# Final units of 256 successive tokens of one batch, stored in 4 KB rows, in an attention and spectral-mixing kernel

## Chip, cores, metric

One core of a Trainium2 chip. The metric is the device time of one execution in microseconds. The kernel before takes 451.3 us (median of 6 runs, 448.56 to 452.69).

## The reference, cut to what matters

```python
# attention: 8 batches, 8 heads, 576 tokens, window 128, ALiBi bias  ->  x [8, 576, 512]
X = rfft(x, axis=1)                      # 64 modes are kept
Y = X[:, :64] mixed per mode with w_r, w_i   # 64 x 2 matrices of 512 x 512 fp32: 134 MB
u = x + irfft(Y)
out = u + relu(u @ w_ch)                 # fp32, 9.44 MB
```

The engines are named as in the profile: PE multiplies matrices, ACT, DVE and GpSimd (POOL in the profile) work on elements, SP issues transfers (DMA). PSUM is the memory that PE writes its results to. The kernel has three stretches. Attention runs to about 130 us. Then the weights stream in and PE multiplies them with the spectra as they land; beside this, x is already projected with w_ch and kept as XW. After the last weight come 18 "final units" of 256 token rows each: `mm` gathers u @ w_ch, ACT takes the relu into `r`, `yy` gathers u, DVE adds the two into `o`, and SP stores `o`. In a "pooled" unit GpSimd adds x to `r`, so PE need not add it into `yy`.

## The kernel before

```python
units = []                                    # before: a unit is one tile of 128 tokens
for bp in range(B // 2):                      # of two batches, b and b + 1
    units += [(2 * bp, st) for st in range(FULL)]
    if bp % 2:
        units.append((2 * bp - 2, FULL))      # the 64 last tokens of four batches
...
def begin(j):                                 # brings XW into PSUM
    ...
        for row in range(2):
            nc.tensor.matmul(
                mm[ROWS[row], n], lhsT=ident[ROWS[n], ROWS[n]],
                rhs=XW[ROWS[n], j, row], start=True, stop=False, skip_group_check=True,
            )

def channels(j):                              # adds the high modes' channel rows
    ...
        for row in range(2):
            spread(mm[:, n], row, b + n, 1, st, row)

def spread(dst, half, b, hf, st, tok):
    row = ROWS[(b % 2) ^ (1 - hf)]            # the batch's parity picks the row half of PE
    nc.tensor.matmul(
        dst[ROWS[half]], lhsT=FT[row, b % 2, tokens(st, tok)], rhs=ZW[row, b // 2, hf],
        start=False, stop=True, skip_group_check=True,
    )
...
def activate(j):                              # begin, channels, relu; for pooled units
    ...                                       # GpSimd adds x to r
def finish(j):
    ...  # add_tokens(j) unless pooled (x through PE), finish_tokens(j), DVE add, store
        nc.sync.dma_start(
            out=out[b + c.start : b + c.stop, st * P : (st + 1) * P].rearrange(
                "b p e -> p b e"), in_=o[:, c])       # 2 KB rows
...
for step in ("a0 f0 a1 f1 a2 a3 f2 a7 f7 a9 a5 f3 f5 a4 f9 a6 a11 f6 f4 a10 a14 f10 "
             "a15 f11 a8 f14 f8 a13 f15 a16 f16 f13 a17 f17 a12 f12").split():
    {"a": activate, "f": finish}[step[0]](int(step[1:]))
```

In `begin` and `channels`, n picks the row half of the PE array and `row` the column half. The four 64x64 matmuls of each step thus lie in four different quadrants.

The softmax here doesn't subtract the row's maximum and nothing guards it: scores larger than these inputs give would overflow.

Of the kernel before, what the change touches and what calls it, by code (L numbers as in the profile page):

```python
# [10 lines left out]
FP32 = mybir.dt.float32  # L11
# [3 lines left out]
ALU = mybir.AluOpType  # L15
# [91 lines left out]
class _Attention:  # L107
# [71 lines left out]
    def inverse_table(self):  # L179

        nc = self.nc
        NM = self.F.shape[2] // 2
        for sts in (range(FULL), (FULL,)):
            ps = self.ps.tile([P, 2, 512], FP32, tag="sc", bufs=2)
            for par in range(2):
                for k in range(4):
                    c0 = NM // 2 * (k % 2) + NM * (1 - (k // 2 + par) % 2)
                    for st in sts:
                        n = P if st < FULL else TAIL
                        nc.tensor.matmul(  # L190
                            ps[32 * k : 32 * k + 32, par, st % FULL * P : st % FULL * P + n],
                            lhsT=self.F[:n, st, c0 : c0 + 32], rhs=self.ident[:n, :n],
                            start=True, stop=True, tile_position=(0, 32 * k),
                        )
            w = P * FULL if len(sts) > 1 else TAIL
            nc.scalar.copy(self.FT[:, :, sts[0] * P : sts[0] * P + w], ps[:, :, :w])
# [203 lines left out]
def kernel(  # L400
# [128 lines left out]
    with ExitStack() as mctx:  # L529
# [14 lines left out]
        def late_end(acc, g, n):  # L544
# [4 lines left out]
            patch([(nc.gpsimd, b) for b in range(2 if g == LAST else 0, B)],  # L549
# [70 lines left out]
        def tokens(st, half):  # L620
            o = st * P + (64 * half if st < FULL else 0)
            return slice(o, o + 64)

        def spread(dst, half, b, hf, st, tok):

            row = ROWS[(b % 2) ^ (1 - hf)]
            nc.tensor.matmul(  # L627
                dst[ROWS[half]], lhsT=FT[row, b % 2, tokens(st, tok)], rhs=ZW[row, b // 2, hf],
                start=False, stop=True, skip_group_check=True,
            )  # L630

        units = []
        for bp in range(B // 2):
            units += [(2 * bp, st) for st in range(FULL)]
            if bp % 2:
                units.append((2 * bp - 2, FULL))

        def token_tiles(j):
            b, st = units[j]
            return x[:, b : b + 2, st] if st < FULL else x[:, b + 1 : b + 4 : 2, FULL]  # L640
# [3 lines left out]
        def transposed(j):  # L644
            src = token_tiles(j)
            tr = lps.tile([P, 2, 4, P], BF16, tag="tr", name="tr")
            for n in range(2):
                for dt in range(4):
                    nc.tensor.transpose(tr[:, n, dt], src[:, n, dt * P : (dt + 1) * P], ident)  # L649
            xTs[j] = pool.tile([P, 2, 4, P], BF16, tag="xT", name="xT")  # L650
            nc.vector.tensor_copy(xTs[j], tr)  # L651
# [6 lines left out]
        def project(j):  # L658

            b, st = units[j]  # L660
# [4 lines left out]
            for n in range(2):  # L665
                mm = ps.tile([P, DM], FP32, tag="my", bufs=2, name="my")
                for dt in range(4):
                    for half in range(2):
                        lhsT = xT[:, half, dt, ROWS[n]] if st < FULL else xT[:, n, dt, ROWS[half]]
                        nc.tensor.matmul(  # L670
                            mm[ROWS[half]], lhsT=lhsT, rhs=wch[:, dt],
                            start=(dt == 0), stop=False, skip_group_check=True,
                        )
                mms.append(mm)
            for n in range(2):
                for half in range(2):
                    spread(mms[n], half, b + half + (2 * n if st == FULL else 0), 0, st, n)
            for n in range(2):
                nc.scalar.copy(XW[:, j, n], mms[n])  # L679
            if j + 1 < len(units):  # L680
                transposed(j + 1)

        POOLED, HALVES, FIRST = (3, 4, 9, 11, 13, 14, 15), (0, 1, 2, 3, 7, 12), (0, 1)
# [10 lines left out]
        def begin(j):  # L694
# [4 lines left out]
            for n in range(2):  # L699
                if units[j][1] == FULL:  # L700
                    nc.tensor.matmul(mm[:, n], lhsT=pairs, rhs=XW[:, j, n],
                                     start=True, stop=False, skip_group_check=True)
                    continue
                for row in range(2):
                    nc.tensor.matmul(  # L705
                        mm[ROWS[row], n], lhsT=ident[ROWS[n], ROWS[n]],
                        rhs=XW[ROWS[n], j, row], start=True, stop=False, skip_group_check=True,
                    )

        def channels(j):  # L710

            mm, b, st = mms[j][0], *units[j]
            for n in range(2):
                if st == FULL:
# [3 lines left out]
                for row in range(2):  # L718
                    spread(mm[:, n], row, b + n, 1, st, row)

        def last_rows(ps, j, rows):

            st = units[j][1]
            for n in range(2):
                nc.tensor.matmul(ps[:, n], lhsT=FM[:, n, st * P : (st + 1) * P], rhs=rows,  # L725
# [20 lines left out]
        def add_tokens(j):  # L746

            yy = yys[j][0]
            for n in range(2):
                nc.tensor.matmul(yy[:, n], lhsT=ident if units[j][1] < FULL else pairs,  # L750
                                 rhs=token_tiles(j)[:, n],
                                 start=True, stop=False, skip_group_check=True)

        def finish_tokens(j):

            yy, b, st = yys[j][0], *units[j]
            for n in range(2):
                if st < FULL:
                    nc.tensor.matmul(  # L759
                        yy[:, n], lhsT=FT[:, n, st * P : (st + 1) * P], rhs=Z[:, b + n],  # L760
# [9 lines left out]
        def finish(j):  # L770

            b, st = units[j]
            if j == 0:
                last_rows(yys[0][0], 0, heads["yq"])
# [6 lines left out]
            (yy, slot), r = yys.pop(j), rs.pop(j)  # L781
            o = heads["out"].tile([P, 2, DM], FP32, tag="o", bufs=5, name="o")
            for c in parts(j):
                nc.vector.tensor_tensor(out=o[:, c], in0=yy[:, c], in1=r[:, c], op=ALU.add)  # L784
                if st < FULL:
                    nc.sync.dma_start(
                        out=out[b + c.start : b + c.stop, st * P : (st + 1) * P].rearrange(
                            "b p e -> p b e"),
# [14 lines left out]
        for g in range(NM // 4):  # L803
# [5 lines left out]
            for i in range(8):  # L809
# [34 lines left out]
                if k == K1 - 1:  # L844
# [13 lines left out]
                    FM = right.tile([P, 2, 2 * P], BF16, name="FM")  # L858
                    nc.gpsimd.memset(FM, 0.0)
                    for b in range(2):  # L860
                        nc.gpsimd.dma_start(
                            out=FM.rearrange("(k v) b s -> k v b s", v=16)[:, b, b],
                            in_=FT[64 * b + 56 : 64 * b + 64, b, : 2 * P],
                        )
# [46 lines left out]
        patch([(nc.sync, 0), (nc.sync, 1)], yq, LAST, lambda b: Z[:, b])  # L911
        patch([(nc.sync, 2)] + [(nc.gpsimd, b) for b in (3, 4, 5, 6)], yq, LAST, lambda b: Z[:, b], 6)
# [17 lines left out]
        channel_rows([(nc.sync, 0), (nc.sync, 1)] + [(nc.gpsimd, b) for b in range(2, B)])  # L930
        patch([(nc.gpsimd, 7)], yq, LAST, lambda b: Z[:, b], 6)

        for step in ("a0 f0 a1 f1 a2 a3 f2 a7 f7 a9 a5 f3 f5 a4 f9 a6 a11 f6 f4 a10 a14 f10 "
                     "a15 f11 a8 f14 f8 a13 f15 a16 f16 f13 a17 f17 a12 f12").split():
# [31 lines left out]
```

## Time and profile before

| mark in the profiled run of the kernel before | us |
|---|---|
| start of the last tile's normalisation in x (taken as the end of attention) | 131.0 |
| first matmul of the last channel product, `zl` | 416.85 |
| first store issued | 420.48 |
| end of the last matmul | 443.75 |
| end of the span | 450.4 |

`zl` follows directly on the last weight, so "`zl` to the end" is the final stage: 33.55 us. Its marks, first from the chain that ended last (start, us, what), then from the order of time (start, us, engine, line, what):

```profile
416.85 1.15 PE zl L569 x8
...
420.48 16.80 SPq L786 DMA_DIRECT2D out_dram<-o  x17
...
445.02 1.27 SPq L786 DMA_DIRECT2D out_dram<-o  x2
```

The last row is the last pair of stores. The page, the windows and the chain of this kernel are shown in the prediction.

### The profile page before, as it was taken

How to read it: one execution, taken by the hardware profiler on the slowest of the kernel's cores; microseconds unless marked ns; L12 is line 12 of the kernel's file. 1: busy time of each engine (PE TensorE's matmuls, PEld its weight loads, DVE VectorE, ACT ScalarE, POOL GpSimd, SP SyncE). 2: the span in 40 equal slices, each digit the busy share in tenths (PEclk: the TensorE clock that was granted, in tenths of full speed). 3: DMA queues.
4: the chain of work that ended last, by engine and by line, in shares of the span. 5: the costliest groups of instructions: out<-in, count | busy, mean ns of one | idle time of the engine just before them, and what ended most of it. 6: DMA issues, size and time to landing. Idle time of an engine off the chain costs nothing. (4 is left out here: it accounts for less than half of the span.)

```text
span 450.4 us, 8021 instructions
## 1 busy us (share of the span) xinstructions
PE 362.3 (80%) x3314; PEld 193.1 (43%) x3314; DVE 177.0 (39%) x323; ACT 152.7 (34%) x196; POOL 73.9 (16%) x130
## 2 busy tenths in 40 slices
PE   4789899999968275776674766999999998877994
PEld 3457676777755032221222233544444443332331
DVE  7878699999752011010100132121212212220684
ACT  6859799999820000000000010211122110110772
POOL 8600000011512010200000000000000000054881
PEclk9989899999999659565659799999999999999998
DMA  8999999999999999999999999999999999995597
GB/s 282 310 310 319 302 232 303 321 311 263 212 266 319 316 260 314 326 372 427 418 421 421 423 422 419 420 421 420 421 418 421 421 420 421 420 399 206 197 358 295
DMA packets 53768, 157.03 MB, mean 349 GB/s; under 512 B 5205, under 2 KB 24421, under 8 KB 41317
## 3 DMA queue, kind: packets, MB, share of 16 engines
q1 hardware_dynamic: 47908, 140.56, 81.2%
q0 software_dynamic: 5824, 15.97, 18.1%
q8 instruction: 26, 0.43, 0.4%
q14 instruction: 10, 0.07, 0.0%
HBM read 162.53 MB, written 9.44 MB: 382 GB/s over the span
## 5 line engine op out<-in xcount | busy, mean ns | idle before, releaser
L832 PE MATMUL acc<-w,XC 128*32 128x512 bf16 x456 | 130.3, 451 | 42.5 <-DMA w<-in_moe_w_i_dram 22.1
L832 PEld LDWEIGHTS <-XC 128*32 128x32 bf16 x508 | 59.8, 139 | 127.5 <-issue 94.2
L294 ACT ACTIVATE att<-sc 128x1024 bf16<-128x1024 f32 x64 | 64.0, 1031 | 10.2 <-PE sc L284 10.2
L604 ACT CAST ZW<-zw 128x512 bf16<-128x512 f32 x8 | 4.7, 585 | 162.4 <-PE zw L602 162.4
L576 DVE TENSOR_SCALAR yq<-acc 128x512 bf16<-128x512 f32 x13 | 8.9, 688 | 104.6 <-PE acc L832 104.6
L679 ACT CAST XW<-my 128x512 bf16<-128x512 f32 x36 | 19.3, 589 | 75.4 <-PE my L627 75.4
L617 POOL DMA_DIRECT2D Z<-yq x19 | 9.7, 519 | 214.1 <-issue 207.7
L331 PE MATMUL av<-vb,att 128*128 128x132 bf16 (+1 forms) x576 | 39.0, 219 | 5.7 <-DVE x L347 3.9
L331 PEld LDWEIGHTS <-att 128*128 128x128 bf16 x704 | 37.2, 99 | 11.2 <-DVE x L347 8.2
L651 DVE COPY xT<-tr 128x1024 bf16<-128x1024 bf16 x18 | 12.5, 692 | 69.7 <-PE tr L649 69.7
L670 PE MATMUL my<-wch,xT 128*64 128x512 bf16 x288 | 34.5, 382 | 0.8 <-DVE xT L651 0.8
L256 ACT COPY qkT<-tp 128x1152 bf16<-128x1152 bf16 x30 | 33.5, 1116 | 3.2 <-PE tp L250 2.5
L284 PE MATMUL sc<-qkT 64*64 64x256 bf16 (+2 forms) x640 | 26.0, 271 | 2.1 <-ACT qkT L256 1.2
L347 DVE TENSOR_TENSOR x<-av,rec 128x640 bf16<-128x640 f32 x32 | 26.4, 824 | 1.1
L784 DVE TENSOR_TENSOR o<-yy,r 128x512 f32<-128x512 f32 (+1 forms) x24 | 21.7, 953 | 6.3 <-ACT r L741 4.6
L284 PEld LDWEIGHTS <-qkT 64*64 64x64 bf16 x640 | 15.0, 111 | 20.1 <-issue 17.1
L670 PEld LDWEIGHTS <-xT 128*64 128x64 bf16 x288 | 14.8, 109 | 18.9 <-issue 6.9
L271 PE MATMUL sc<-bias,ident 128*128 128x512 bf16 x64 | 21.4, 420 | 1.4 <-ACT att L294 1.4
L233 DVE CAST vb<-vr 64x1024 bf16<-64x1024 f32 x32 | 22.2, 694 | 0.3
L606 DVE CAST Z<-z 64x512 bf16<-64x512 f32 x16 | 11.0, 689 | 25.0 <-PE z L599 24.9
L741 ACT ACTIVATE r<-mm 128x512 f32<-128x512 f32 (+1 forms) x24 | 18.1, 811 | 7.4 <-PE mm L627 4.2
L305 DVE TENSOR_TENSOR att<-att,mask 128x1024 bf16<-128x1024 bf16 x32 | 20.6, 684 | 0.0
(133 smaller groups left out, 372.7 us busy)
## 6 DMA issues: line engine op xcount, KB each, us to landing
w<-in_moe_w_i_dram SPq DMA_DIRECT2D x52, 1024.0 KB, 18.0
w<-in_moe_w_r_dram SPq DMA_DIRECT2D x45, 1024.0 KB, 17.9
qr<-in_q_dram SPq DMA_DIRECT2D x16, 576.0 KB, 9.4
kr<-in_k_dram SPq DMA_DIRECT2D x16, 576.0 KB, 7.1
vr<-in_v_dram SPq DMA_DIRECT2D x64, 128.0 KB, 6.5
w<-in_moe_w_r_dram POOLq DMA_DIRECT2D x16, 512.0 KB, 17.3
out_dram<-o SPq DMA_DIRECT2D x10, 512.0 KB, 3.8
out_dram<-o SPq DMA_DIRECT2D x16, 256.0 KB, 3.5
```

The costliest lines, as they stand in the source:

```text
L233: nc.vector.tensor_copy(self.vb[u % 2][row, :, :, :, W * half : W * half + D], src[row, :2])
L256: (self.nc.vector.tensor_copy if u < 2 and w == "q" else self.nc.scalar.copy)(dst.rearrange("q h (p j) -> q h p j", j=TPP), tp.rearrange(" ...
L271: nc.tensor.matmul(sc[:, e], lhsT=self.ident, rhs=self.bias[:, hv].rearrange("p j n -> p (j n)"), start=True, stop=False, skip_group_check ...
L284: nc.tensor.matmul(sc[64 * half : 64 * half + 64, e, j * 256 + c0 : j * 256 + c0 + n], lhsT=qkT[row, 1, h, k0 + j : k0 + P : 2], rhs=qkT[r ...
L294: self.nc.scalar.activation(self.att[u % 2][:, kt * 8 * P : (kt + 1) * 8 * P], sc.rearrange("p e n -> p (e n)"), AF.Exp, scale=1.0 / math. ...
L305: nc.vector.tensor_tensor(out=rows, in0=rows, in1=self.table[:, heads], op=ALU.mult)
L331: nc.tensor.matmul(bank[:, qt * W : qt * W + rhs[j].shape[1]], lhsT=att[:, o : o + P], rhs=rhs[j], start=(n == 0 and j == 0), stop=(n == l ...
L347: nc.vector.tensor_tensor(out=self.x[:, b, :, cs].rearrange("p t (h d) -> p h t d", h=2), in0=tiles[:, :, :, :D], in1=rec.unsqueeze(-1).br ...
L670: nc.tensor.matmul(mm[ROWS[half]], lhsT=lhsT, rhs=wch[:, dt], start=(dt == 0), stop=False, skip_group_check=True,)
L679: nc.scalar.copy(XW[:, j, n], mms[n])
L784: nc.vector.tensor_tensor(out=o[:, c], in0=yy[:, c], in1=r[:, c], op=ALU.add)
L832: nc.tensor.matmul(into[32 * (i // 2) : 32 * (i // 2) + 32], lhsT=window[a], rhs=w[a], start=(ri == 0 and a == 0), stop=(ri == (m > 0) and ...
```

## The change

The intent: a unit covers 256 successive tokens of one batch, two per partition, so one partition's two rows are one run of 4 KB in the output. x lies in tiles of 128 tokens, so it has to be permuted: on PE by strided columns of the identity, and for the pooled units, where GpSimd reads x directly, in place and ahead of time, in the weight stream. The columns of the inverse table take the same order.

```diff
@@ units
-            units += [(2 * bp, st) for st in range(FULL)]
+            units += [(2 * bp + i, r) for i in range(2) for r in range(FULL // 2)]
@@ new: the permutation on PE
+        def paired(dst, src, n, first):
+            for h in range(2):
+                nc.tensor.matmul(dst[ROWS[h]], lhsT=ident[:, n::2], rhs=src[:, h],
+                                 start=True, stop=not first, skip_group_check=first)
@@ project(j), in the weight stream
+            if j in POOLED:
+                src = token_tiles(j)
+                both = [ps.tile([P, DM], FP32, tag="my", bufs=2, name="my") for _ in range(2)]
+                for n in range(2):
+                    paired(both[n], src, n, False)
+                for n in range(2):
+                    nc.vector.tensor_copy(src[:, n], both[n])
@@
-        POOLED, HALVES, FIRST = (3, 4, 9, 11, 13, 14, 15), (0, 1, 2, 3, 7, 12), (0, 1)
+        POOLED, HALVES, FIRST = (2, 5, 7, 13, 14, 15), (0, 1, 3, 4, 6, 9), (0, 1)
@@ begin(j)
-                for row in range(2):
-                    nc.tensor.matmul(
-                        mm[ROWS[row], n], lhsT=ident[ROWS[n], ROWS[n]],
-                        rhs=XW[ROWS[n], j, row], start=True, stop=False, skip_group_check=True,
-                    )
+                nc.tensor.matmul(mm[:, n], lhsT=ident if units[j][1] < FULL else pairs,
+                                 rhs=XW[:, j, n], start=True, stop=False, skip_group_check=True)
@@ channels(j)
-                for row in range(2):
-                    spread(mm[:, n], row, b + n, 1, st, row)
+                spread(mm[:, n], b, 1, r, n)        # 64 rows x 128 columns, one row half
@@ add_tokens(j)
-                nc.tensor.matmul(yy[:, n], lhsT=ident if units[j][1] < FULL else pairs,
-                                 rhs=token_tiles(j)[:, n], ...)
+                if units[j][1] < FULL:
+                    paired(yy[:, n], token_tiles(j), n, True)
+                    continue
@@ finish(j)
-                        out=out[b + c.start : b + c.stop, st * P : (st + 1) * P].rearrange(
-                            "b p e -> p b e"),
+                        out=out[b, 2 * r * P : 2 * (r + 1) * P].rearrange(
+                            "(p j) e -> p j e", j=2)[:, c],
@@ after the last weight, before the steps
+        add_tokens(1)
+        finish_tokens(1)
@@ the order of the steps
+        for step in ("a0 f0 a1 f1 a3 a2 f3 a9 f9 a4 a15 f4 f2 a10 a7 f10 f15 a12 a13 f12 f7 "
+                     "a11 a5 f11 a16 f13 a14 f16 a8 f5 f14 a17 f8 f17 a6 f6").split():
(cut: the inverse table's columns, the table FM, the projection in 128-column matmuls,
 `finish` of unit 1, which now only adds its last rows, the order of the last patches)
```

More of the change, by code (lines that the diff above doesn't have):

```diff
@@ L189, in inverse_table @@
                         n = P if st < FULL else TAIL
+                        to = ps[32 * k : 32 * k + 32, par]
+                        if st < FULL:
+                            to = to[:, st // 2 * 2 * P : st // 2 * 2 * P + 2 * P].rearrange(
+                                "k (j t) -> k j t", j=2)[:, :, st % 2 * 64 : st % 2 * 64 + 64]
+                            rhs = self.ident.rearrange("k (t j) -> k j t", j=2)
+                        else:
+                            to, rhs = to[:, :n], self.ident[:n, :n]
                         nc.tensor.matmul(
-                            ps[32 * k : 32 * k + 32, par, st % FULL * P : st % FULL * P + n],
-                            lhsT=self.F[:n, st, c0 : c0 + 32], rhs=self.ident[:n, :n],
+                            to, lhsT=self.F[:n, st, c0 : c0 + 32], rhs=rhs,
                             start=True, stop=True, tile_position=(0, 32 * k),
@@ L548, in late_end @@
             nc.vector.tensor_scalar_mul(yq[rows], acc[rows], 2.0 / S)
-            patch([(nc.gpsimd, b) for b in range(2 if g == LAST else 0, B)],
+            patch([(nc.gpsimd, b) for b in range(1 if g == LAST else 0, B)],
                   yq, g, lambda b: Z[:, b], 0, 2 * n)
@@ L618, in patch, with columns, spread @@
                                 in_=rows.rearrange("(k v) e -> k v e", v=16)[lo:hi, b])
-        def tokens(st, half):
-            o = st * P + (64 * half if st < FULL else 0)
-            return slice(o, o + 64)
-        def spread(dst, half, b, hf, st, tok):
+        def columns(r, j):
+            return slice((2 * r + j) * P, (2 * r + j + 1) * P)
+        def spread(dst, b, hf, r, j):
             row = ROWS[(b % 2) ^ (1 - hf)]
             nc.tensor.matmul(
-                dst[ROWS[half]], lhsT=FT[row, b % 2, tokens(st, tok)], rhs=ZW[row, b // 2, hf],
+                dst, lhsT=FT[row, b % 2, columns(r, j)], rhs=ZW[row, b // 2, hf],
                 start=False, stop=True, skip_group_check=True,
@@ L638, in token_tiles @@
         def token_tiles(j):
-            b, st = units[j]
-            return x[:, b : b + 2, st] if st < FULL else x[:, b + 1 : b + 4 : 2, FULL]
+            b, r = units[j]
+            return x[:, b, 2 * r : 2 * r + 2] if r < FULL else x[:, b + 1 : b + 4 : 2, FULL]
         xTs = {}
@@ L645, in transposed @@
             src = token_tiles(j)
-            tr = lps.tile([P, 2, 4, P], BF16, tag="tr", name="tr")
+            tr = lps.tile([P, 4, 2, P], BF16, tag="tr", name="tr")
             for n in range(2):
                 for dt in range(4):
-                    nc.tensor.transpose(tr[:, n, dt], src[:, n, dt * P : (dt + 1) * P], ident)
-            xTs[j] = pool.tile([P, 2, 4, P], BF16, tag="xT", name="xT")
-            nc.vector.tensor_copy(xTs[j], tr)
+                    nc.tensor.transpose(tr[:, dt, n], src[:, n, dt * P : (dt + 1) * P], ident)
+            xTs[j] = pool.tile([P, 4, 2 * P], BF16, tag="xT", name="xT")
+            nc.vector.tensor_copy(xTs[j], tr.rearrange("p d n t -> p d (n t)"))
+        def paired(dst, src, n, first):
+            for h in range(2):
+                nc.tensor.matmul(dst[ROWS[h]], lhsT=ident[:, n::2], rhs=src[:, h],
+                                 start=True, stop=not first, skip_group_check=first)
         def warm():
@@ L658, in project @@
         def project(j):
-            b, st = units[j]
+            b, r = units[j]
             if j == 0:
@@ L667, in project @@
                 for dt in range(4):
+                    if r < FULL:
+                        nc.tensor.matmul(mm, lhsT=xT[:, dt, n::2], rhs=wch[:, dt],
+                                         start=(dt == 0), stop=False, skip_group_check=True)
+                        continue
                     for half in range(2):
-                        lhsT = xT[:, half, dt, ROWS[n]] if st < FULL else xT[:, n, dt, ROWS[half]]
                         nc.tensor.matmul(
-                            mm[ROWS[half]], lhsT=lhsT, rhs=wch[:, dt],
-                            start=(dt == 0), stop=False, skip_group_check=True,
+                            mm[ROWS[half]],
+                            lhsT=xT[:, dt, P * n + 64 * half : P * n + 64 * half + 64],
+                            rhs=wch[:, dt], start=(dt == 0), stop=False, skip_group_check=True,
                         )
@@ L675, in project @@
             for n in range(2):
+                if r < FULL:
+                    spread(mms[n], b, 0, r, n)
+                    continue
                 for half in range(2):
-                    spread(mms[n], half, b + half + (2 * n if st == FULL else 0), 0, st, n)
+                    bb = b + half + 2 * n
+                    row = ROWS[(bb % 2) ^ 1]
+                    nc.tensor.matmul(
+                        mms[n][ROWS[half]], lhsT=FT[row, bb % 2, FULL * P :],
+                        rhs=ZW[row, bb // 2, 0], start=False, stop=True, skip_group_check=True,
+                    )
             for n in range(2):
                 nc.scalar.copy(XW[:, j, n], mms[n])
+            if j in POOLED:
[5 more added lines that the diff above has]
+                    nc.vector.tensor_copy(src[:, n], both[n])
             if j + 1 < len(units):
                 transposed(j + 1)
-        POOLED, HALVES, FIRST = (3, 4, 9, 11, 13, 14, 15), (0, 1, 2, 3, 7, 12), (0, 1)
+        POOLED, HALVES, FIRST = (2, 5, 7, 13, 14, 15), (0, 1, 3, 4, 6, 9), (0, 1)
         mms, yys, rs = {}, {}, {}
@@ L699, in begin @@
             for n in range(2):
-                if units[j][1] == FULL:
-                    nc.tensor.matmul(mm[:, n], lhsT=pairs, rhs=XW[:, j, n],
-                                     start=True, stop=False, skip_group_check=True)
-                    continue
-                for row in range(2):
-                    nc.tensor.matmul(
-                        mm[ROWS[row], n], lhsT=ident[ROWS[n], ROWS[n]],
-                        rhs=XW[ROWS[n], j, row], start=True, stop=False, skip_group_check=True,
-                    )
+                nc.tensor.matmul(mm[:, n], lhsT=ident if units[j][1] < FULL else pairs,
+                                 rhs=XW[:, j, n], start=True, stop=False, skip_group_check=True)
         def channels(j):
-            mm, b, st = mms[j][0], *units[j]
+            mm, b, r = mms[j][0], *units[j]
             for n in range(2):
-                if st == FULL:
+                if r == FULL:
                     nc.tensor.matmul(mm[:, n], lhsT=FC, rhs=ZW[:, b // 2 + n, 1],
@@ L717, in channels @@
                     continue
-                for row in range(2):
-                    spread(mm[:, n], row, b + n, 1, st, row)
+                spread(mm[:, n], b, 1, r, n)
         def last_rows(ps, j, rows):
-            st = units[j][1]
             for n in range(2):
-                nc.tensor.matmul(ps[:, n], lhsT=FM[:, n, st * P : (st + 1) * P], rhs=rows,
+                nc.tensor.matmul(ps[:, n], lhsT=FM[:, columns(units[j][1], n)], rhs=rows,
                                  start=False, stop=True, skip_group_check=True)
@@ L749, in add_tokens @@
             for n in range(2):
-                nc.tensor.matmul(yy[:, n], lhsT=ident if units[j][1] < FULL else pairs,
-                                 rhs=token_tiles(j)[:, n],
+                if units[j][1] < FULL:
+                    paired(yy[:, n], token_tiles(j), n, True)
+                    continue
+                nc.tensor.matmul(yy[:, n], lhsT=pairs, rhs=token_tiles(j)[:, n],
                                  start=True, stop=False, skip_group_check=True)
         def finish_tokens(j):
-            yy, b, st = yys[j][0], *units[j]
+            yy, b, r = yys[j][0], *units[j]
             for n in range(2):
-                if st < FULL:
+                if r < FULL:
                     nc.tensor.matmul(
-                        yy[:, n], lhsT=FT[:, n, st * P : (st + 1) * P], rhs=Z[:, b + n],
+                        yy[:, n], lhsT=FT[:, b % 2, columns(r, n)], rhs=Z[:, b],
                         start=j in POOLED, stop=True, skip_group_check=True,
@@ L770, in finish @@
         def finish(j):
-            b, st = units[j]
-            if j == 0:
-                last_rows(yys[0][0], 0, heads["yq"])
+            b, r = units[j]
+            if j in FIRST:
+                last_rows(yys[j][0], j, heads["yq"])
             else:
@@ L780, in finish @@
                 finish_tokens(j)
-            (yy, slot), r = yys.pop(j), rs.pop(j)
+            (yy, slot), res = yys.pop(j), rs.pop(j)
             o = heads["out"].tile([P, 2, DM], FP32, tag="o", bufs=5, name="o")
             for c in parts(j):
-                nc.vector.tensor_tensor(out=o[:, c], in0=yy[:, c], in1=r[:, c], op=ALU.add)
-                if st < FULL:
+                nc.vector.tensor_tensor(out=o[:, c], in0=yy[:, c], in1=res[:, c], op=ALU.add)
+                if r < FULL:
                     nc.sync.dma_start(
-                        out=out[b + c.start : b + c.stop, st * P : (st + 1) * P].rearrange(
-                            "b p e -> p b e"),
+                        out=out[b, 2 * r * P : 2 * (r + 1) * P].rearrange(
+                            "(p j) e -> p j e", j=2)[:, c],
                         in_=o[:, c],
@@ L857 @@
                     XW = right.tile([P, len(units), 2, DM], BF16, name="XW")
-                    FM = right.tile([P, 2, 2 * P], BF16, name="FM")
+                    FM = right.tile([P, FULL * P], BF16, name="FM")
                     nc.gpsimd.memset(FM, 0.0)
-                    for b in range(2):
-                        nc.gpsimd.dma_start(
-                            out=FM.rearrange("(k v) b s -> k v b s", v=16)[:, b, b],
-                            in_=FT[64 * b + 56 : 64 * b + 64, b, : 2 * P],
-                        )
+                    nc.gpsimd.dma_start(out=FM.rearrange("(k v) s -> k v s", v=16)[:, 0],
+                                        in_=FT[56:64, 0, : FULL * P])
                     FI = right.tile([P, 2, P], BF16, name="FI")
@@ L910 @@
                                   trs[i][:, 2 * i : 2 * i + 2, 96:])
-        patch([(nc.sync, 0), (nc.sync, 1)], yq, LAST, lambda b: Z[:, b])
-        patch([(nc.sync, 2)] + [(nc.gpsimd, b) for b in (3, 4, 5, 6)], yq, LAST, lambda b: Z[:, b], 6)
+        token_rows = partial(patch, rows=yq, g=LAST, dst=lambda b: Z[:, b])
+        token_rows([(nc.sync, b) for b in (1, 2, 3)] + [(nc.gpsimd, b) for b in (4, 5, 6)], lo=6)
         yw = F[:, : DM // (2 * NM)].rearrange("p a b -> p (a b)")
@@ L929 @@
         channel_rows = partial(patch, rows=yw, g=LAST, dst=lambda b: ZW[:, b // 2, 1])
-        channel_rows([(nc.sync, 0), (nc.sync, 1)] + [(nc.gpsimd, b) for b in range(2, B)])
-        patch([(nc.gpsimd, 7)], yq, LAST, lambda b: Z[:, b], 6)
-        for step in ("a0 f0 a1 f1 a2 a3 f2 a7 f7 a9 a5 f3 f5 a4 f9 a6 a11 f6 f4 a10 a14 f10 "
-                     "a15 f11 a8 f14 f8 a13 f15 a16 f16 f13 a17 f17 a12 f12").split():
+        channel_rows([(nc.sync, 1), (nc.sync, 2)] + [(nc.gpsimd, b) for b in range(3, B)])
+        add_tokens(1)
+        finish_tokens(1)
+        token_rows([(nc.gpsimd, 7)], lo=6)
+        channel_rows([(nc.gpsimd, 0)])
+        token_rows([(nc.gpsimd, 0)])
+        for step in ("a0 f0 a1 f1 a3 a2 f3 a9 f9 a4 a15 f4 f2 a10 a7 f10 f15 a12 a13 f12 f7 "
+                     "a11 a5 f11 a16 f13 a14 f16 a8 f5 f14 a17 f8 f17 a6 f6").split():
             {"a": activate, "f": finish}[step[0]](int(step[1:]))
```

## The prediction

> **What bounds the kernel now.** I read the page's 40 slices first, then the windows, then the chain that ended last, then the order of time inside one unit.
>
> ```profile
> span 450.4 us, 8021 instructions
> PE   4789899999968275776674766999999998877994
> PEclk9989899999999659565659799999999999999998
> DMA  8999999999999999999999999999999999995597
> GB/s 282 310 310 319 302 232 303 321 311 263 212 266 319 316 260 314 326 372 427 418 421 421 423 422 419 420 421 420 421 418 421 421 420 421 420 399 206 197 358 295
> ```
>
> A slice is 450.4 / 40 = 11.3 us. From slice 18 to 35 (about 205 to 405 us) the DMA engines are full at some 420 GB/s: the weight stream. Slices 36 and 37 are a hole: the last weights are used and the first results are not yet out. The last slices are the final stage, 9.44 MB of results. The change leaves attention alone (only the inverse table's columns are reordered), so two stretches count: the stream's spare room on PE, and the stage after the last weight. The windows, with columns PE, PEld, DVE, ACT, POOL busy (count), clock, DMA share, GB/s:
>
> ```profile
> 320.00:350.00 30.00, 29.66 (x220) 14.39 (x219) 5.25 (x9) 6.44 (x12) 0.00 (x0) 1.00 1.01 419
> 380.00:412.00 32.00, 23.25 (x103) 10.08 (x103) 6.70 (x11) 2.92 (x5) 9.17 (x18) 1.00 1.00 393
> 421.00:444.00 23.00, 22.52 (x174) 7.48 (x167) 19.36 (x22) 16.27 (x21) 16.40 (x10) 1.00 0.94 343
> ```
>
> In the final stage (421 to 444) PE is busy 22.52 of 23 us and DMA 0.94. Two resources are near full, so I ask the chain which one leads. Its pieces (start, us, what) through two pairs of units:
>
> ```profile
> 428.79 0.41 PE mm L705 x4
> 429.19 0.22 PE mm L627 x4
> 429.41 0.54 PE yy L750 x2
> 429.95 0.86 PE yy L759 x4
> 430.81 0.34 PE mm L705 x4
> 431.15 0.22 PE mm L627 x4
> 431.37 0.22 PE mm L705 x4
> 431.58 0.22 PE mm L627 x4
> 431.80 0.55 PE yy L750 x2
> 432.35 0.43 PE yy L759 x2
> ```
>
> It is PE work end to end, from 420.82 to 438.4 almost without a break. The reader is to see three prices here. A 128x128 matmul of 512 columns costs 0.43 / 2 = 0.215 us. Four 64x64 matmuls that lie in four different quadrants cost 0.22 together. A change between the two forms adds about 0.11 (0.34 against 0.22, 0.54 against 0.43). So PE sets the pace and the output DMA follows just behind it.
>
> **What the Trainium skill says.** "TensorEngine Tiling (Array Packing)", Key Properties: tiles work independently and in parallel, and changing the tiling mode drains the engine. The trace agrees on both: four quadrants in 0.22 us, and the 0.11 us at each change. "TensorE: Matmul & The Clock Gate", Back-to-back issue gap, gives 131 ns for a sustained N=512 matmul and about 216 isolated; this trace has 215, and I use that. "DMA: Bandwidth & Descriptors", Why small descriptors are slow, names a fixed cost of about 3 cycles per packet. The trace points the same way: in 435 to 440 us the results go out in 2 KB packets at 378 GB/s with DMA share 1.02, while the 8 KB weight rows reach 420 at the same share.
>
> **The change part by part.**
>
> *Packets.* A unit now covers 256 successive tokens, row 2p and 2p+1 on partition p, so an unsplit store has 4 KB runs. From 378 and 420 GB/s a 2 KB packet takes 16 x 2048 / 378 = 87 ns and an 8 KB one 312; a line through both puts 4 KB at about 162 ns, 405 GB/s (an estimate). But 6 regular units are still stored in halves (2 KB runs) and the 2 tail units are as before: 10 of 18 gain, 10 x 0.524 MB x (1/378 - 1/405) = 0.9 us. That is all there is to win in transfer time, and only if DMA leads.
>
> *PE in a final unit.* Before, the activation was 4 quadrant matmuls to bring XW in (0.22) and 4 for the channel rows (0.22): the two batches sat in the two row halves and the two token halves in the two column halves, so all four ran at once. After, both tiles are of one batch. Bringing XW in is 2 full 128x128 (0.43), and the channel rows are 2 matmuls of 64 rows x 128 columns in the same row half, hence one after the other (0.43). Half of the array idles and nothing runs beside it: +0.42 per regular unit. Adding x as 4 matmuls of 128x64, two at a time, costs the same 0.43 as before, the token matmuls also 0.43. Forms now alternate 128x128, 64x128, 128x64, 128x128, so an unpooled unit has three or four changes instead of two. POOLED falls from 7 units to 6, so the unpooled regular units after the first two go from 7 to 8.
> I add the order of the 34 steps after units 0 and 1. Activation: 0.43 + 0.54 (0.97; 1.08 where it follows another form). Unpooled finish 0.54 + 0.54. Pooled finish 0.43 or 0.54. The tail units: 0.86 to activate, 1.29 to finish. The 14 regular activations come to 14.2, the 8 unpooled finishes to 8.6, the 6 pooled to 2.7, the two tail units to 4.3: 29.8 us. The same stretch before is 443.77 - 420.82 = 22.95 in the chain. So +6.8 us, if a change of rows alone or columns alone drains as the change of both does. If it doesn't, some 40 x 0.11 = 4.4 less.
>
> *The head.* Before the last weight PE prepares unit 0: 413.24 to 414.76 before; with the new forms +0.7 us, on the path because the last weight's matmuls wait for nothing but PE there. After it, begin and channels of unit 1 (0.56 in the chain) become 0.97, and adding x and tokens of unit 1 (1.08) now comes ahead of the first `last_rows`. Unit 1's finish is then 0.43 instead of 0.86. To the end of unit 1: 0.97 + 1.08 + 4 x 0.43 = 3.77 against 2.83, +0.9. The first store is issued later than 420.48, by some 2 us.
>
> *The stream.* Projection: 16 matmuls of 128x64, two at a time (1.85 us), become 8 of 128x128: the same. The spreads there ran as two pairs and become two singles: the same 0.43. New are the six pooled units: PE must wait until ACT has emptied both banks, permute (0.43), then DVE copies back. I estimate 1.3 us of PE each (ACT's two copies take 1.07), 7.8 together. PE already trails the weights there (no wait for a weight from 277 to 377 us), but a load takes about 17 us from issue to landing with 1 MB each 2.5 us, so the queue stays fed through 12 us of lag. From 377 on PE waits 9.5 us in total for weights and the like: that absorbs 7.8, just. Cost on the path: 0, up to 2 at worst.
>
> *The end.* PE-bound, the last stores meet an emptier queue and land in 2.5 instead of 3.5 us: -1.0.
>
> Sum: 6.8 + 0.7 + 0.9 - 1.0 = +7.4 us with all drains, +3 without any of the added ones.
>
> **The rivals.** (1) The output DMA leads, PE's extra work is hidden, and 4 KB runs win 0.9 us, perhaps 2 with fewer bubbles: about 450. For it: DMA share 1.02 in 435 to 440. Against: the chain, and PE's 22.52 of 23. (2) The permutation overruns the stream's spare time, the last weight is used late, and it comes on top: 461 or more. For it: 7.8 of 9.5 is tight, and DVE holds the banks 1.4 us more. Against: 17 us from issue to landing is some seven loads queued, so DMA should not run dry. (3) Row-half and column-half forms switch for nothing: 455. Nothing in the trace shows such a change alone, except 128x32 to 128x64 in the stream, which costs about 0.1.
>
> **Range and chances.** 451.8 + 7.4 = 459; halfway between the drain and the no-drain sums it is 457. I say 457.5, and 452 to 461. The low end leaves room for rival 1, as the new order of steps, the new pooled set and the new order of patches look tuned for this form. Slower by over 2% means above 460.8, which needs rival 2 on top: 0.14. Faster by over 2% (under 442.7) would need 9 us out of a stage whose DMA alone takes 9.44 MB / 405 = 23 us: 0.02. Within 2%: 0.84.
>
> **What would show it.** Right: in the final stage the chain is PE throughout, from about 422 to 450 us, DMA share falls to 0.75 to 0.85, activation pairs take 0.86 to 1.08 instead of 0.44, the first store is issued near 422.5, the last weight's matmuls start within 2 us of before. Wrong: the windows of the final stage keep DMA at 0.95 or above while PE shows waits (rival 1); waits for weights vanish through 412 and the last weight's matmuls start after 417 (rival 2); no 0.11 us between the forms (rival 3).

## The result, and the profile after

The changed kernel takes 457.45 us (median of 6 runs, 456.72 to 459.33) against 451.28. The ratio is 1.015, with a 95% interval of 1.0112 to 1.0188. A second measurement on another chip, the control below, gave 1.0189. The change costs 6 to 9 us.

The slices of the changed kernel's page (11.4 us each here):

```profile
span 454.6 us, 7681 instructions
PE   4688999999866455656565668999999999999995
DMA  8999999999999999999999999999999999991677
GB/s 280 314 320 322 308 304 286 312 296 259 213 303 317 290 306 317 335 386 425 422 420 422 422 421 420 420 418 422 420 420 420 420 373 403 423 393 35 256 290 282
```

Before, the last two slices ran at 358 and 295 GB/s; now the last three run at 256, 290 and 282, with DMA at 6 and 7 tenths. PE stands at 9 through the end, but for the last slice. The windows (PE, PEld, DVE, ACT, POOL busy, clock, DMA share, GB/s):

```profile
380.00:412.00 32.00, 31.38 (x146) 12.50 (x146) 8.87 (x15) 2.93 (x5) 9.53 (x19) 1.00 0.95 381
421.00:448.00 27.00, 26.92 (x124) 8.17 (x122) 17.71 (x19) 14.90 (x17) 12.79 (x6) 1.00 0.73 283
```

In the final stage PE is busy 26.92 of 27 us and the DMA share has fallen from 0.94 to 0.73. In the stream's last stretch PE's idle time is gone as well: 31.38 of 32 us busy, against 23.25 before. The chain that ended last, through two activations and what follows them:

```profile
428.13 0.43 PE mm L730 x2
428.56 0.53 PE mm L632 x2
429.09 0.54 PE mm L730 x2
429.63 0.54 PE mm L632 x2
430.17 0.55 PE yy L661 x4
430.72 0.97 PE yy L782 x4
```

L730 is `begin` and L632 the channel rows. Two activations take 0.43 + 0.53 + 0.54 + 0.54 = 2.04 us; in the chain before, the pair from 430.81 took 0.34 + 0.22 + 0.22 + 0.22 = 1.00. Half the number of instructions takes twice the time, because the instructions no longer run beside each other, and each change between `begin` and the channel rows shows as 0.11 on top of 0.43. L661 adds x as 128x64 and L782 the token rows of two units as 128x128: 0.97 for four is 0.86 and, again, 0.11 for the change of form.

Where the time went, stage by stage, in the first profiles of both kernels and in the control's:

| stretch, us | before | after | after, control |
|---|---|---|---|
| start to the end of attention | 131.0 | 128.2 | 130.4 |
| from there to `zl` | 285.85 | 286.20 | 286.36 |
| `zl` to the first store | 3.63 | 5.03 | 5.03 |
| `zl` to the end of the last matmul | 26.90 | 35.01 | 35.02 |
| end of the last matmul to the end | 6.65 | 5.19 | 5.12 |
| **`zl` to the end** | **33.55** | **40.20** | **40.14** |

The final stage repeats to within 0.11 us (40.09 to 40.20 in the four profiles that leave its PE work alone: this one, the control, e2 and e3). The attention stretch varies by up to 3 us between profiles of kernels that all have the same attention (127.8 to 131.0 over the profiles); I did not find out why. The profiled run of the changed kernel had a short one, which is why its span is only 4.2 us longer. So in the experiments I judge by "`zl` to the end" first, and by the ratio second. Among the variants of the changed kernel, only e1 and e4 have ratios clear of both measurements of the changed kernel; the smaller effects below rest on one profile each.

### The profile page after: what moved, and what is told of

Same layout as the page of the kernel before. It is cut to its first block, busy times and chain, and to the rows that moved or that the text cites. A ratio compares the mean times of both kernels' runs of the same rounds, so it can differ in the third digit from the quotient of the medians. Undisturbed runs are those within 1.5% of the kernel's fastest.

```text
span 454.6 us, 7681 instructions
## 1 busy us (share of the span) xinstructions
PE 366.0 (81%) x3138; PEld 189.7 (42%) x3138; DVE 184.4 (41%) x335; ACT 152.8 (34%) x196; POOL 72.1 (16%) x129
## 5 line engine op out<-in xcount | busy, mean ns | idle before, releaser
L855 PE MATMUL acc<-w,XC 128*32 128x512 bf16 x456 | 126.4, 439 | 44.9 <-DMA w<-in_moe_w_r_dram 27.6
L855 PEld LDWEIGHTS <-XC 128*32 128x32 bf16 x508 | 58.5, 139 | 119.7 <-issue 83.2
L680 PE MATMUL my<-wch,xT 128*128 128x512 bf16 x128 | 30.4, 380 | 0.8 <-DVE xT L656 0.8
L277 PE MATMUL sc<-bias,ident 128*128 128x512 bf16 x64 | 19.9, 394 | 1.4 <-ACT att L300 1.4
L530 POOL COPY gate<-x 1x1 bf16<-1x1 bf16 x11 | 5.8, 526 | 85.7 <-DVE x L353 85.7
```

The costliest lines, as they stand in the source:

```text
L277: nc.tensor.matmul(sc[:, e], lhsT=self.ident, rhs=self.bias[:, hv].rearrange("p j n -> p (j n)"), start=True, stop=False, skip_group_check ...
L680: nc.tensor.matmul(mm, lhsT=xT[:, dt, n::2], rhs=wch[:, dt], start=(dt == 0), stop=False, skip_group_check=True)
L855: nc.tensor.matmul(into[32 * (i // 2) : 32 * (i // 2) + 32], lhsT=window[a], rhs=w[a], start=(ri == 0 and a == 0), stop=(ri == (m > 0) and ...
```

## The experiments

Eleven kernels ran, each profiled, all timed in five rounds against the kernel before. Theory: PE leads the final stage, and the cost is the activations' lost concurrency and their changes of form. Rivals: the output DMA or the packet size matters, the permutation delays the stream, the order of steps is the cause.

| run | results | ratio to before (95%) | `zl` to the end, us |
|---|---|---|---|
| c_after | right | 1.0189 (1.0154 to 1.0224) | 40.14 |
| e1_quadrants | wrong | 1.0032 (1.0001 to 1.0062) | 34.64 |
| e3_2kb | right | 1.0159 (1.0128 to 1.0191) | 40.09 |
| e4_quadrants_2kb | wrong | 1.0043 (1.0007 to 1.0078) | 34.66 |
| e2_no_permute | wrong | 1.0133 (1.0101 to 1.0166) | 40.16 |
| e5_row_halves | wrong | 1.0107 (1.0065 to 1.0149) | 37.30 |
| e6_padded | right | 1.0140 (1.0093 to 1.0186) | 38.21 |
| e7_before_full | wrong | 1.0123 (1.0080 to 1.0165) | 38.40 |
| e8_pairs | right | 1.0140 (1.0116 to 1.0164) | 40.58 |
| e9_before_pool8 | right | 1.0109 (1.0081 to 1.0136) | 37.63 |
| e10_four_pairs | right | 1.0131 (1.0098 to 1.0165) | 38.51 |

The first four shared one chip, the next four another, e8 and e9 a third, e10 a fourth.

**c_after**, the changed kernel again.

> Control: the changed kernel again, beside the others of this call. Every theory: 1.015 of the kernel before (about 457.5 us); from the first matmul of the last channel product (zl) to the end of the span 40.2 us, as in its first profile (33.55 in the kernel before).

459.11 us, ratio 1.0189: a little above the first measurement, whose interval overlaps. The final stage is the same to 0.06 us.

**e1_quadrants**: the activation's old forms in the changed kernel.

```diff
 begin:    -  mm[:, n] <- ident x XW[:, j, n]
           +  for row in range(2): mm[ROWS[row], n] <- ident[ROWS[n], ROWS[n]] x XW[ROWS[n], j, row]
 channels: -  spread(mm[:, n], b, 1, r, n)
           +  for h in range(2): mm[ROWS[h], n] <- FT[ROWS[n], b % 2, 64 columns of half h]
           +                       x ZW[ROWS[n], b // 2, int(n == b % 2)]
```

> The changed kernel with the activation's eight 64x64 quadrant matmuls of the kernel before put back (results wrong on purpose: data of the other half and order). Theory (PE leads the final stage, and the lost quadrant concurrency with its changes of form is the cost): activations of the 14 regular units fall from 14.2 to about 7.2 us, the heads of units 0 and 1 by 0.4 each, so the last matmul comes 7 to 8 us earlier, 1 to 1.5 us of it given back to the output queue; from zl to the end 33.5 to 34.5 us, time 450.5 to 452. Rival (permutation in the stream, order of steps or the store pattern is the cost): still 456 to 458.

452.20 us, ratio 1.0032 where the control beside it has 1.0189; 34.64 us from `zl` to the end, 0.14 above the range expected. The last matmul ends 28.42 us after `zl` instead of 35.02: 6.6 earlier, not 7 to 8. The chain of this kernel, two activations:

```profile
423.21 0.34 PE mm L735 x4
423.55 0.22 PE mm L751 x4
423.77 0.22 PE mm L735 x4
423.98 0.21 PE mm L751 x4
```

0.99 us for what took 2.04. With order, permutation, pooled set and 4 KB stores left as they are, this gives back 5.5 of the 6.6 us of the final stage. What remains against the kernel before (34.64 against 33.55) is about as large as the delay of the first store, 4.62 after `zl` instead of 3.63, but no run tests this: the order of steps and the one more unpooled unit are still in it too.

**e3_2kb**: two transfers of 2 KB rows per unit instead of one.

```diff
-  nc.sync.dma_start(out=...[:, c], in_=o[:, c])
+  for n in range(c.start, c.stop): nc.sync.dma_start(out=...[:, n], in_=o[:, n])
```

> The changed kernel, computing as it does, but each unit stored as two transfers of 2 KB rows. Theory (PE leads, the output DMA has slack at share 0.73): within 0.5 us of the control, from zl to the end 40.0 to 40.7. Rival (packet size is worth time here): 0.9 us or more slower than the control.

40.09 us against the control's 40.14, and a ratio of 1.0159 against 1.0189 with overlapping intervals. In time it is 457.35 us, 1.8 below the control and so outside the 0.5 expected, but away from the rival and within the spread of the runs. The 4 KB rows show no gain in the changed kernel.

**e4_quadrants_2kb**: both edits together.

> Quadrants put back and 2 KB rows together. Where PE is quick again, the DMA share of the final stage is near 0.9 and packet size may count: theory says 0 to 0.9 us slower than e1_quadrants (10 units x 0.524 MB x (1/378 - 1/405) us per kB as the ceiling); a rival in which the 4 KB rows were the change's real gain says over 1.5 us.

34.66 against 34.64 us. Even with PE quick again the packet size does not show in the time. It does show in the rate: between `zl` + 4 us and the last matmul, 2 KB rows moved 325 GB/s at a DMA share of 0.88, the mix with 4 KB rows 329 at 0.86, that is 369 against 383 GB/s per full share. It is a gain of about 3.6%, with shares read to 0.01, on an engine that does not lead.

**e2_no_permute**: the block `if j in POOLED:` of `project` left out.

> The changed kernel without the in-place permutation of the six pooled units (results wrong on purpose). Theory (the stream's spare PE time takes it in): waits of PE for weights come back between 300 and 412 us, time 0 to 1 us under the changed kernel's 457.5. Rival 2 of the prediction (the permutation delays the end of the stream): 2 to 6 us faster.

The final stage is unchanged (40.16). From the end of attention to `zl` it takes 285.14 us, 1.1 less than the changed kernel's 286.20 and 286.36; waits of PE for weights are back (8.5 us from 290 us to `zl`, 0.0 in the changed kernel's first profile). But this stretch also varies by itself: over the nine profiles with the permutation in it (both of the changed kernel, e1, e3 to e6, e8, e10) it takes 285.60 to 286.36 us. So the permutation costs some 0.5 to 1.2 us, as far as one profile can tell, and not the 2 to 6 of the rival. In time e2 (1.0133) can't be told from the changed kernel's first measurement. The windows of 370 to 380 us, first the changed kernel, then this one:

```profile
370.00:380.00 10.00, 10.00 (x57) 4.19 (x54) 0.69 (x1) 1.83 (x4) 0.00 (x0) 1.00 0.95 360
```

```profile
370.00:380.00 10.00, 8.87 (x41) 3.78 (x41) 2.57 (x5) 0.59 (x1) 0.00 (x0) 1.00 1.02 424
```

After three pooled units in a row PE trails so far that weight loads are issued too late: 360 GB/s instead of 424 for 10 us, which is 10 x (424 - 360) / 424 = 1.5 us of stream (an estimate). The control has the same dip, 355 GB/s from 372 to 382 us. How much of it is on the path is what e2 bounds.

**e5_row_halves**: the two channel matmuls of a unit in different row halves.

```diff
-  spread(mm[:, n], b, 1, r, n)
+  rows = ROWS[(b % 2) ^ n]
+  mm[:, n] <- FT[rows, b % 2, columns(r, n)] x ZW[rows, b // 2, 1 - n]
```

> The changed kernel, but the two channel matmuls (64 rows x 128 columns) of a unit take different row halves instead of one (results wrong on purpose); same number, size and form. Theory: they run at once, 0.22 instead of 0.43 us, 16 units, so the last matmul comes 3.4 us earlier and the time falls by 2.8 to 3.4 us to about 454.3. Rival (two row tiles do not overlap in this form, or PE does not lead): within 0.5 us of the changed kernel.

```profile
425.97 0.43 PE mm L730 x2
426.40 0.32 PE mm L742 x2
```

The two channel matmuls take 0.32 instead of 0.53 us, the final stage 37.30 instead of 40.20: 2.9 us, as expected. The median is 455.03, 0.7 above the figure expected. Nothing but the row half of every second matmul, and the data that lie there, differs, so this is the price of having both tiles of a unit in one row half. The comparison with the reference passed this kernel, although half the rows take the low modes twice and the high modes not at all: the error lies under its tolerance, so a pass is no proof here.

**e6_padded**: channel matmuls over all 128 rows, with zeros in the other half of the table.

```diff
+  FZ = right.tile([P, 2, FULL * P], BF16, name="FZ")   # FT with the other half zero
-  spread(mm[:, n], b, 1, r, n)
+  mm[:, n] <- FZ[:, b % 2, columns(r, n)] x ZW[:, b // 2, 1]
   (batch 0's last patches move behind step a2)
```

> The changed kernel with channel matmuls of the full 128x128 form, through a table whose other half is zero (results right); the patches of batch 0 move behind unit 2's activation so that nothing waits for them. Same streamed columns, no change of form inside an activation. Theory: about 20 changes of form at 0.11 us go, and three in the head: 2.2 to 2.6 us faster than the changed kernel, about 455. Rival (a change of rows alone does not drain, the 0.11 has another cause): within 0.5 us of it.

```profile
424.08 0.43 PE mm L741 x2
424.51 0.43 PE mm L730 x2
```

38.21 us: 2.0 less than the changed kernel, a little under the 2.2 expected. In time it is 456.13 us against the 455 expected, and its ratio overlaps the changed kernel's. The same number of columns streams; in the activations only the change between 128x128 and 64x128 is gone, and with it the 0.11 us (the moved patches are in the 2.0 us as well). So a change of rows alone does cost it, which the prediction had left open. For a change of columns alone (128x64 to 128x128) the changed kernel's chain shows the same: 0.54 us for the two token matmuls of a unit behind its x.

**e7_before_full**: the mirror of e1, the new activation forms in the kernel before (`begin` with the whole identity, channel rows as 64x128 in the low half).

> The kernel before with nothing of the change but its activation forms: two 128x128 matmuls to bring XW in and two 64x128 in one row half for the channel rows, instead of eight 64x64 quadrants (results wrong on purpose). Theory: 14 units x 0.42 us plus about 0.9 us for units 0 and 1, less 1 us at the end: 5 to 6.5 us slower than before, about 457. Rival (the output DMA leads and hides PE's work): 0 to 2 us slower.

38.40 against 33.55 us: 4.85 slower in this stretch, and 5.6 us (1.23%) in time, inside the 5 to 6.5 expected. The chain of this kernel:

```profile
425.43 0.43 PE mm L700 x2
425.87 0.54 PE mm L711 x2
```

No other part of the change is in this kernel, so the activation forms alone make most of the loss. The last matmul ends 6.4 us later after `zl` (33.29 against 26.90), and 1.5 of these come back behind it (5.1 us to the end instead of 6.65): about a quarter is given back while the last stores land. So PE leads in the kernel before too, with the output DMA close behind.

**e8_pairs** and **e10_four_pairs** try to win the concurrency back in the new layout with right results: two units, one of an even and one of an odd batch, are activated together and their channel matmuls alternate between the row halves.

```diff
+  for j in both: begin(j)
+  for n in range(2):
+      for j in both: spread(mms[j][0][:, n], b of j, 1, r of j, n)
+  for j in both: relu(j)
```

> The changed kernel with results right: twelve of the regular units are activated in pairs of one even and one odd batch (3 and 9, 4 and 2, 10 and 15, 12 and 13, 7 and 14, 11 and 5), their four channel matmuls alternating between the two row halves; the order of steps follows. Theory: a pair costs 0.43 + 0.43 + 0.11 + 0.43 = 1.40 us of PE instead of 2.05, six pairs save 3.9 us, less some 1 to 1.5 us of PE waiting for both activation buffers: from zl to the end 36.5 to 38 us against 40.2, time about 454.5, still 3 us or more behind the kernel before. Rival (alternating halves of two units do not overlap, or the order of steps matters more): 40 us or above.

It missed: 40.58 us, and 456.64 (four runs) where 454.5 was expected. The pairs did overlap (four channel matmuls in 0.54 us in its chain), but my order of steps put two GpSimd additions late: the chain ends through GpSimd's last two (2.1 us each) and DVE's, not through PE.

> The changed kernel with its own order of steps, results right; only the four neighbouring activations that are of one even and one odd batch (4 and 15, 10 and 7, 12 and 13, 11 and 5) alternate their channel matmuls between the row halves. Theory: 4 x 0.65 = 2.6 us less PE work, little of it lost to waits because the order is kept: from zl to the end 37.6 to 38.6 against 40.2, time 1.5 to 2.6 us under the changed kernel's. Rival (what e8_pairs lost was not its order: pairing itself brings nothing): 40 us or above.

With the changed kernel's own order, 38.51 us: inside the range expected, 1.7 less than the changed kernel. In time its median is 455.95, 1.5 under the changed kernel's first median, though on another chip and with overlapping ratios. Some of the 2.6 us of PE work saved goes to waits for both activations of a pair: ACT stands in its chain with 1.0 to 1.5 us after three of the four pairs.

**e9_before_pool8**: the kernel before with unit 5 pooled as well.

> The kernel before with one more pooled unit (5): it needs no permutation there, so PE saves one addition of x, 0.54 us, and GpSimd takes 2.1 us more. If PE leads the kernel before, from zl to the end falls from 33.55 to about 33.0 to 33.3; the output DMA close behind caps it. Rival (GpSimd's extra addition delays the finishes behind it): 34 us or more. In time within noise of the kernel before either way.

```profile
428.08 2.36 DVE L784 TENSOR_TENSOR o<-yy,r 128x1024 f32<-128x1024 f32 x2 [3.03 <-POOL r L744]
429.36 0.59 PE L750 MATMUL yy<-x,ident 128*128 128x512 bf16 x2 [2.66 <-DVE o L784]
```

37.63 us, 4 us worse, and 1.1% in time, where I had expected noise: the rival was right. In this order of time the brackets say what an engine waited for. DVE waits 3.03 us for GpSimd's addition and PE in turn 2.66 us for DVE to free its buffer. So GpSimd had no room left for an eighth addition in the kernel before. No version I ran beats it, so none is proposed.

## Why the prediction was right, step by step

The predicted 457.5 us stands against a measured 457.45 and, in the control, 459.11. The terms of its sum, against the profiles:

| term | predicted | measured | from |
|---|---|---|---|
| steps after unit 1, on PE | 22.95 to 29.8, +6.8 | 30.1, +7.1 | chain: 419.34 to 449.43 |
| unit 1's head after `zl` | +0.9 | +0.95 (3.78 against 2.83) | chain: 415.56 to 419.34 |
| unit 0 ahead of the last weight | +0.7 | +0.54 (2.33 against 1.79), not seen in the stretch around it | order of time: first transpose of the partial rows to the last weight's first matmul |
| stream | 0, up to 2 | some 0.5 to 1.2 | e2 against nine profiles with the permutation |
| last matmul to the end | -1.0 | -1.5 | table of stretches |
| full drains or none | between | full drains | rows: e6, 0.43 instead of 0.54; columns: L782 behind L661, 0.54 |

- **PE leads.** Right. The chain is PE almost throughout, and the final stage moved with PE's work in e1, e5, e6, e7 and e10. In the kernel before, the chain goes twice through DVE and ACT (433.88 to 435.28 and 438.42 to 440.77 us), which the prediction's "PE work end to end" passes over. PE has other work meanwhile (busy 22.52 of 23 us), so its 22.95 us may still be read as PE's.
- **Lost quadrants.** Right in place and size. e1 gives 5.5 us back by undoing the activation forms, and e7 loses 4.85 by doing them alone. Within this, e5 prices the channel rows' lost overlap at 2.9 us and e6 the row-only changes of form at 2.0.
- **Packets.** The prediction allowed them 0.9 us if DMA led. It does not lead, and e3 and e4 find nothing in the time. Its line through 378 and 420 GB/s compares stores with loads, so it was not a clean price of the packet; e4 against e1 is the only comparison of stores alone.
- **The permutation.** The extra PE time per pooled unit was predicted at 1.3 us. In the order of time, first the unit of the kernel before, then a pooled one of the changed kernel:

```profile
330.09 1.92 PE L670 MATMUL my<-wch,xT 128*64 128x512 bf16 x16
331.94 0.62 PE L627 MATMUL my<-ZW,FT 64*64 64x512 bf16 x4
332.49 0.62 PE L649 MATMUL tr<-ident,x 128*128 128x128 bf16 x8
```

```profile
353.49 1.90 PE L680 MATMUL my<-wch,xT 128*128 128x512 bf16 x8
355.32 0.60 PE L632 MATMUL my<-ZW,FT 64*128 64x512 bf16 x2
356.38 0.90 PE L661 MATMUL my<-x,ident 128*64 128x512 bf16 x4 [0.46 <-ACT XW L702]
357.21 0.62 PE L654 MATMUL tr<-ident,x 128*128 128x128 bf16 x8
```

From the projection to the transposes it is 2.40 us in the one and 3.72 in the other: 1.32 more, with the wait for ACT's evacuation inside. One statement beside it did not hold: "DMA should not run dry" was wrong for some 10 us after the last three pooled units.
- **The end.** Right in kind and short in size: stores of 256 KB now land in 2.4 us (median) instead of 3.5.

- **The signs set in advance.** The chain, the activations (0.96 to 1.08 us) and the 0.11 us came as stated. The DMA share fell to 0.73, just past the 0.75 to 0.85. The first store came 1.4 us later after `zl` (5.03 against 3.63), not 2. The last weight's work began earlier, not later: `zl` stands at 414.40 against 416.85, because attention was 2.8 us shorter in this run. The waits for weights did vanish (0.0 us, 0.9 in the control), one half of rival 2's sign; the late `zl`, its other half, did not come.

For the final stage the terms give 6.8 + 0.9 - 1.0 = 6.7 us; measured are 40.20 - 33.55 = 6.65. The 0.7 us for unit 0 does not show: from attention to `zl` the kernel before takes 285.85 us, and 286.37 in e9, which has the same stream; the changed kernel takes 286.20 and 286.36. Nor do the rows of unit 0 and of the permutation add up to that stretch; what offsets them is open.

So the mechanism and its largest term were right, but that the figure hit to 0.1 us is luck. With all drains the sum was 459; I stated 457.5 because I had put half the weight on drains that might not exist. They do, and the first measurement still fell on the lower figure. The sum was also set on 451.8, the time of the profiled run, and not on the median of 451.28. Runs of one kernel spread over 4 us, and the two measurements differ from the kernel before by 6.2 and 8.7 us, so times alone could not have told 457 from 459.

## What to carry to other kernels

Before a layout is changed for the sake of a transfer, look at which engine the chain names: here PE led and DMA followed just behind, so quicker transfers were worth nothing, and of the 8.1 us by which PE's last matmul came later 6.65 reached the end. On PE, count columns streamed one after the other, not instructions: two small matmuls in one row half cost twice what four in four quadrants do, and a layout that puts all of a unit's data into one row half gives that concurrency away. Work moved into a stretch with spare time is cheap only while the stretch has some left. Here some 0.5 to 1.2 us of the 7.8 reached the path, but three such units in a row still starved the stream for a moment.

## What the Trainium skill lacked or had wrong

- "TensorEngine Tiling (Array Packing)", Key Properties: says that a change of tiling mode drains the engine, with no size. Here a change costs 0.11 us, and it is paid for a change of rows alone (128x128 to 64x128: 0.54 instead of 0.43 us for two matmuls; e6 without it: 0.43) and for one of columns alone (128x64 to 128x128: 0.54).
- The same page, Performance Considerations: advises tiling for small contractions, but gives no time for 64-row matmuls that share a row half. Here two in one row half took 0.53 us and two in different halves 0.32 (e5), each with one change of form in it; two full ones with such a change took 0.54.
- "TensorE: Matmul & The Clock Gate", Back-to-back issue gap: gives about 131 ns as the sustained spacing of 512-column matmuls and 216 as that of a single one. Here eight full 128x128 matmuls in a row took 1.72 us (from 417.62 us in the changed kernel's chain), 215 ns each, at a granted clock of 1.00.
- "DMA: Bandwidth & Descriptors", Bandwidth: no figure measured on trn2 for stores by row size. Here stores of 2 KB rows moved 369 GB/s per full DMA share, a mix with 4 KB rows 383.
